# First feed-forward block of an S5 layer kernel: w1 loaded by rows, 14 sums open at once, a norm's scales on GpSimd

## The chip, the cores and the metric

One core of one Trainium2 chip runs the whole program. The metric is the device time of one execution in microseconds (us): the median of three runs of the kernel before is 155.63 us (155.48 to 155.71). TensorE (PE) multiplies matrices and adds into eight PSUM banks, VectorE (DVE), ScalarE (ACT) and GpSimd (POOL) do the elementwise work, and SyncE (SP) issues nearly all DMAs. Each engine takes its own instructions in order; between engines an instruction waits on semaphores.

## The reference

The input x is 2048 tokens of 448 values, in bf16. Everything starts from one layer norm without weights and runs in two branches:

```python
xn  = layernorm(x)                                  # eps 1e-5
# branch A: a diagonal complex state space model
dt  = exp(log_dt);  Lam_bar = exp(dt * Lam)         # Lam = Lambda_re + 1j Lambda_im, 448 states
Bu  = xn @ ((Lam_bar - 1) / Lam * B).T              # complex, 448 x 448
h_t = Lam_bar * h_(t-1) + Bu_t                      # over the 2048 tokens
s   = 2 * Re(h @ C.T) + xn * Dskip
# branch B: a second layernorm on xn and a feed-forward block
g   = silu(gelu(layernorm(xn) @ w1 + b1) @ w2 + b2) # w1: 448 x 1792, w2: 1792 x 448
out = x + s * g
```

## The kernel before

The tokens are cut into four groups `g` of 512. A group has two blocks `b` of 256 tokens, and a block two parities `par`: row pairs 2p and 2p+1 lie on partition p, so that a tile is 128 partitions by 448. All of x, w1, w2, B and C stay in SBUF.

Work is recorded as tasks in a class `Plan`: a task is a list of instructions of one engine with the names of what it reads and writes. `link` turns the names into dependencies, and `emit` issues the tasks in a list written out by hand, `ORDER` (numbers stand for tasks without a tag, names for tagged ones); `SECOND` lists the tasks that go to the second of their two possible engines. Before a task's first instruction `emit` puts the semaphore waits of all its dependencies. DMAs are tasks too, nearly all on SP's queue (a few on ACT's); copies are issued on line 90, transposing DMAs on line 89.

The head, up to 19.6 us, is what the change is about:

- `ldw1` (L333) loads w1 in four column chunks, `CH = ((0, 4), (4, 4), (8, 4), (12, 2))` in units of 128 columns. Rows 0 to 383 go as 3 x 128 partitions, the last 64 rows as a second DMA. w2 comes in four chunks of rows, the bias b1 in four small loads (`b1b`), w1's last partition 64 of row chunk 3 holds b1 for the first group.
- 28 matmuls of the identity on itself (L828) keep TensorE busy until there is data. They wait for GpSimd's memsets.
- `first_norm` (L386 to L405) does block 0: statistics on VectorE (L393, L394), the scale by Ln and Exp on ScalarE (L396), the normalised block (L398), TensorE transposes (L401) with five dummy matmuls behind them (L403), and copies out of PSUM into `xn2T` (L405). The nine small matmuls of `parameters` (L480 to L484), which turn the state parameters to columns, come ahead of these.
- For block 1 of group 0, `ln_stats` (L379, L383) and `ln_scale` (L412) run on VectorE: ten small operations (L422 to L432) take an inverse square root by two Newton steps. `ln_apply` (L448) normalises, TensorE transposes (L464), VectorE copies (L470).
- `mm1_half` (L742) multiplies one block by w1, two column tiles f at a time: for each f the four row chunks d one after another, 8 matmuls of 128x128 by 256 tokens, into a pair of banks (0/1, 2/3, 4/5 in turn), followed by one gelu on ScalarE (L754). Seven pairs for block 0, then seven for block 1.
- `mm2` (L757) follows: 14 matmuls for each (block, parity), which wait for all four w2 chunks before the first; then b2 (L765) and silu (L766).

From group 1 on, `mm1` (L724) does the w1 product for both blocks at once, 512 tokens wide, with row tiling: two products of 64 rows each stand side by side in the array (L728), and the 64 rows left over are copied to both halves. Its gelu is L738. `bu` (L651) multiplies by the transposed B (`BT`, product L654), the scan follows on VectorE (L679), and `ym` (L783) multiplies the states by C (products L792, L795 and L798), then the product with g (L801), the skip and the residual (L804), and the store. `xn2T` and `xnT` of the later groups, `BT` and `Cr` (C transposed) are made by transposing DMAs on SP's queue.

GpSimd and ScalarE work out the angles and powers of the scan (L500 to L519 on GpSimd) between 6 and 16 us. For groups after the first, `ln_scale` runs on GpSimd as two add-multiplies (L422, L423), a power of -0.5 (L424), a multiply and a change of sign (L425, L426), all with one instruction for 4 or 8 columns.

Of the kernel before, what the change touches and what calls it, by code (L numbers as in the profile page):

```python
# [9 lines left out]
BF = dt.bfloat16  # L10
# [7 lines left out]
class Task:  # L18
# [3 lines left out]
    __slots__ = ("eng", "ins", "reads", "writes", "sem", "idx", "deps", "chain", "alts", "tag")  # L22

    def __init__(self, eng, ins, reads, writes, sem):
        self.eng, self.ins, self.reads, self.writes, self.sem = eng, ins, tuple(reads), tuple(writes), sem
        self.deps = set()
        self.chain = False
        self.tag = None
        self.alts = [(eng, ins)]
# [7 lines left out]
class Plan:  # L37
# [55 lines left out]
    def link(self):  # L93
        last, readers = {}, {}
        for t in self.tasks:
            for k in t.reads:
                if k in last:
                    t.deps.add(last[k])
            for k in t.writes:
# [12 lines left out]
    def emit(self):  # L112
# [8 lines left out]
        for t in order:  # L121
# [3 lines left out]
            need = {}  # L125
            for d in t.deps:
                sem, val = done[d]
                if need.get(sem, 0) < val:
                    need[sem] = val
            for sem, val in need.items():  # L130
                if seen.get(sem, 0) < val:
                    eng.wait_ge(self.sems[sem], val)
                    seen[sem] = val
            for k, fn in enumerate(t.ins):
                last = fn(eng)
# [26 lines left out]
10 0 18 22 1 19 23 20 16 15 88 2 21 11 3 9 27 26 12 8 17 14 13 89 24 5 7 90 25 6 4 91 28 96 29 45 97 30 92 98 93 46 31 99 94 47 48 63 103 95  # L162
53 100 32 49 101 54 50 102 33 51 52 106 114 64 44 65 55 108 105 B0 56 116 115 B1 107 109 B2 57 117 58 B3 42 118 38 110 120 39 119 40 144 122
111 121 104 41 60 112 DH 36 123 69 126 59 113 34 67 37 124 305 127 35 154 304 43 128 125 148 132 152 129 66 306 134 307 149 133 310 308 309
311 155 130 193 153 135 312 156 138 131 195 146 140 157 159 139 158 136 147 160 161 275 137 68 316 BF 61 317 62 72 70 167 313 318 73 141 272
314 74 71 169 75 76 287 W0 168 276 W1 170 82 281 171 83 77 273 162 78 410 84 173 86 163 413 W2 284 278 183 315 196 150 184 164 282 417 174
283 412 W3 288 80 79 411 277 185 414 165 H10 279 166 143 415 H12 416 274 177 285 418 364 151 518 517 H11 519 365 187 368 172 366 145 369 175
H13 191 516 81 319 367 H15 419 186 521 176 370 422 320 374 523 178 390 188 371 522 233 85 87 179 289 189 375 H16 520 286 322 420 192 180 423
H14 323 234 524 393 376 424 235 377 190 372 236 421 237 373 321 199 378 200 238 241 528 324 242 203 182 197 239 181 204 H21 198 243 201 H20
240 202 472 425 470 529 325 471 207 247 525 194 473 250 381 251 326 530 244 526 249 245 205 527 252 H23 206 261 H24 142 209 248 476 246 379  # L170
478 253 255 262 208 256 327 210 257 266 258 259 211 328 221 263 267 219 264 260 265 329 212 268 477 220 213 382 254 222 223 384 225 269 226
224 214 229 227 280 215 230 330 270 228 H26 216 231 383 428 217 232 331 218 334 290 333 479 335 387 291 385 386 332 293 388 426 389 H22 427
294 295 297 391 336 292 339 482 298 474 299 483 338 300 337 344 475 429 H30 342 430 353 341 H25 301 296 564 340 496 343 480 565 H31 392 347
345 302 H33 354 355 531 348 394 566 349 481 499 350 358 271 570 359 431 360 346 567 484 351 352 356 361 362 432 380 396 571 433 534 397 395
399 532 434 435 533 400 401 403 303 436 439 440 487 398 441 402 404 485 406 535 448 488 437 536 489 490 438 497 357 449 442 446 498 445 493
447 444 443 451 453 454 363 537 494 491 495 450 492 H32 538 407 459 H34 464 486 460 568 408 461 465 H36 462 569 539 466 452 405 455 500 463
409 576 540 467 H35 593 468 572 501 456 574 469 573 457 458 541 575 502 542 577 545 546 543 503 581 544 547 553 552 554 550 505 582 578 506
583 555 504 507 590 508 548 509 551 549 557 591 579 556 587 510 558 559 580 560 512 561 584 592 562 513 563 511 514 599 588 515 589 596 600
585 594 586 595 603 597 598 601 602 611 604 607 612 605 613 606 608 614 609 610
""".split()]  # L180
SECOND = [int(k) if k.isdigit() else k for k in """
142 143 144 145 146 147 149 161 167 169 197 199 205 207 221 223 227 229 231 284 285 286 391 392 394 395 419 423 428 496 501 524 525 529 590 591 592 594 595 613 W0
# [12 lines left out]
def bass_recurrent_scan__ssm_conv_s5__mixer_channel_mlp__prompt_kernel(  # L195
# [18 lines left out]
    with ExitStack() as es:  # L214
# [3 lines left out]
        ident = SB("ident", [128, 128])  # L218
        mhalf = SB("mhalf", [128, 1, 1], F32)
# [70 lines left out]
        with nc.Block():  # L290

            S0 = -100
            pool(lambda e: e.memset(ident[:], 1.0), [], ["ident"], 0.2, 3 * PINNED)
# [39 lines left out]
            def ldw1(c, prio):  # L333
                a, w = CH[c][0] * 128, CH[c][1] * 128
# [9 lines left out]
            for c in (1, 2, 3):  # L344
                ldw1(c, S1 + 3)
# [487 lines left out]
            for par in range(2):  # L833
                ln_apply(0, 1, par, 1, "only dve", 2 * PINNED + 4)
# [86 lines left out]
```

## Time and profile before

| what | value |
|---|---|
| median of three runs | 155.63 us (155.48 to 155.71) |
| profiled execution | 155.18 us, span 153.1 us, 2.1 us outside the span |
| granted TensorE clock, mean | 1.00 |
| PE busy | 148.4 us of the span, 97% |
| DVE, ACT, POOL busy | 86%, 67%, 31% |
| first matmul, first w1 product, first w2 product | 1.42, 6.50, 19.60 us |
| w1 chunks landed | 6.24, 7.97, 9.49, 10.20 us |
| w2 chunks landed | 16.42, 17.58, 18.77, 19.55 us |
| one transposing DMA on SP's queue | 1.2 to 1.3 us of issue, landing about 3 us after its start |

A row of the timeline gives the start and length in us, the engine, the line, the operation, what is written and read, the tile, the number of instructions, and, in square brackets, the idle time before it with what ended it. The chain of waits goes back from the last instruction to what released each step. The waits list says for each engine and line how long it stood idle and for whom. The profiled execution lies 0.45 us under the median, so a time worked out from its rows is taken against 155.18 and then set to the median.

### The profile page before, as it was taken

Reading aid. Unit: us, or ns where it says so; the run is one execution under the profiler, and the core shown is the slowest. Engines: PE = TensorE matmul, PEld = TensorE weight load, DVE = VectorE, ACT = ScalarE, POOL = GpSimd, SP = SyncE. Lnnn points to the kernel's source line nnn. Section 1 sums busy time; section 2 is a strip of 40 time slices with the busy share of each in tenths; the row PEclk is TensorE's granted clock in tenths of the full one; section 3 lists DMA queues with packets and bytes.
Section 4 is the critical chain, followed back from the end, with each engine's and each line's share of the span. In section 5 each row is a group of like instructions: output and inputs, shape, how many; then the busy total and the mean of one; then the engine's idle time right before and its main releaser. Section 6 shows DMA issues by size and latency. Waiting matters only on the chain.

```text
span 153.1 us, 3017 instructions
## 1 busy us (share of the span) xinstructions
PE 148.4 (97%) x1079; PEld 89.9 (59%) x1079; DVE 131.3 (86%) x275; ACT 102.5 (67%) x175; POOL 47.3 (31%) x122
## 2 busy tenths in 40 slices
PE   6999999999999999999999999999999999999992
PEld 6899945454575555755544556665555665555551
DVE  5879999999988999999859998349699539999784
ACT  3876959999885688798993599841419987244110
POOL 6465896374520004700000079000512920000001
PEclk9999999999999999999999999999999999999999
DMA  4998999996859553000003310042300100010103
GB/s 115 311 259 268 349 175 238 211 187 130 160 88 175 88 103 69 0 2 0 4 1 59 84 40 0 0 96 84 62 2 0 62 0 4 0 62 0 60 0 120
DMA packets 31512, 14.04 MB, mean 92 GB/s; under 512 B 25733, under 2 KB 31113, under 8 KB 31498
## 3 DMA queue, kind: packets, MB, share of 16 engines
q1 hardware_dynamic: 31344, 13.80, 39.5%
q8 instruction: 8, 0.13, 0.4%
q10 hardware_dynamic: 154, 0.06, 0.1%
q14 instruction: 6, 0.05, 0.1%
HBM read 6.20 MB, written 1.84 MB: 53 GB/s over the span
## 4 chain that ended last, share of the span: by engine, by line
PE 85%; SPq 6%; DMA 5%; issue 1%; DVE 1%
PE psum L762 28%; PE psum L728 22%; PE psum L654 15%; PE psum L792 13%; SPq L90 6%; DMA w_sb<-in_B_w_dram 5%; PE psum L795 4%; PE psum L636 3%; PE psum L798 1%; PE psum L642 1%; DVE t L801 0%; DVE tmp L804 0%; PE psum L638 0%; PE psum L644 0%
## 5 line engine op out<-in xcount | busy, mean ns | idle before, releaser
L762 PE MATMUL psum<-w_sb,gT 128*128 128x448 bf16 x224 | 44.3, 353 | 0.1
L728 PE MATMUL psum<-xn2T,w_sb 64*128 64x512 bf16 x294 | 33.9, 378 | 0.0
L762 PEld LDWEIGHTS psum<-w_sb,gT 128*128 128x128 bf16 x224 | 21.8, 98 | 19.8 <-DMA w_sb<-in_B_w_dram 0.4
L738 ACT ACTIVATE gT<-psum,b1f 128x512 bf16<-128x512 f32 x42 | 26.0, 687 | 6.9 <-PE psum L728 6.7
L728 PEld LDWEIGHTS psum<-xn2T,w_sb 64*128 64x128 bf16 x294 | 15.6, 109 | 16.1 <-issue 3.0
L654 PE MATMUL psum<-xnT,BT 128*128 128x256 bf16 x196 | 24.1, 273 | 0.0
L654 PEld LDWEIGHTS psum<-xnT,BT 128*128 128x128 bf16 x196 | 18.4, 98 | 6.5 <-issue 3.3
L766 ACT ACTIVATE g_sb<-o 128x448 bf16<-128x448 f32 x16 | 9.1, 572 | 12.2 <-DVE o L765 12.1
L801 DVE TENSOR_TENSOR t<-psum,g_sb 128x448 bf16<-128x448 f32 (+2 forms) x17 | 10.0, 591 | 5.9 <-PE psum L795 2.8
L679 DVE TENSOR_TENSOR_SCAN s_f<-cw,cur,v_sb 128x256 f32<-128x256 f32 x21 | 14.9, 737 | 0.1
L693 POOL TENSOR_TENSOR cwk<-s_f,ang 128x3 f32<-128x3 f32 x3 | 1.4, 470 | 43.3 <-DVE s_f L679 43.3
L748 PE MATMUL psum<-xn2T,w_sb 128*128 128x256 bf16 x112 | 12.6, 273 | 0.3 <-DVE xn2T L405 0.3
L748 PEld LDWEIGHTS psum<-xn2T,w_sb 128*128 128x128 bf16 x112 | 11.9, 111 | 0.7 <-issue 0.4
L792 PE MATMUL psum<-CZ,h_sb 128*128 128x448 bf16 x56 | 11.9, 353 | 0.0
L765 DVE TENSOR_TENSOR o<-psum,b2bc 128x448 f32<-128x448 f32 x16 | 9.7, 614 | 1.7 <-PE psum L762 1.7
L792 PE MATMUL psum<-CQ,h_sb 128*128 128x448 bf16 (+2 forms) x54 | 10.5, 332 | 0.0
L683 ACT ACTIVATE s_b<-s_f 128x1536 bf16<-128x1536 f32 x4 | 5.9, 1485 | 6.7 <-DVE s_f L679 6.7
L658 ACT ACTIVATE u_sb<-psum 128x512 bf16<-128x512 f32 x12 | 7.2, 598 | 4.6 <-PE psum L654 4.6
L448 DVE TENSOR_SCALAR xn_sb<-x_all,lnw 128x448 bf16<-128x448 bf16 (+1 forms) x30 | 9.9, 364 | 0.3
L754 ACT ACTIVATE gT<-psum 128x512 bf16<-128x512 f32 x14 | 8.2, 592 | 2.7 <-PE psum L748 2.7
L804 POOL TENSOR_TENSOR tmp<-t,xr 128x192 bf16<-128x192 bf16 x1 | 0.5, 548 | 26.3 <-DVE t L801 26.3
L792 PEld LDWEIGHTS psum<-CZ,h_sb 128*128 128x128 bf16 x56 | 5.3, 98 | 5.1 <-issue 0.5
(160 smaller groups left out, 236.9 us busy)
## 6 DMA issues: line engine op xcount, KB each, us to landing
out_dram<-tmp SPq DMA_DIRECT2D x7, 224.0 KB, 1.9
x_all<-in_A_x_dram SPq DMA_DIRECT2D x3, 448.0 KB, 4.7
w_sb<-in_B_w_dram SPq DMA_DIRECT2D x3, 448.0 KB, 7.3
w_sb<-in_B_w_dram SPq DMA_DIRECT2D x3, 384.0 KB, 4.4
Bn<-in_A_B_im_dram SPq DMA_DIRECT2D x1, 336.0 KB, 8.5
Bn<-in_A_B_re_dram SPq DMA_DIRECT2D x1, 336.0 KB, 8.7
x_all<-in_A_x_dram SPq DMA_DIRECT2D x2, 112.0 KB, 2.1
x_all<-in_A_x_dram SPq DMA_DIRECT2D x1, 224.0 KB, 2.7
```

The source lines that it names most:

```text
L90: return e.dma_start(out_ap, in_ap)
L448: on = [("dve", [lambda e, o=o, i=i: e.tensor_scalar(o, i, rs, nb, op0=ALU.mult, op1=ALU.add) for o, i in pairs], 0.4, 0.12), ("act", [lam ...
L654: fns = [lambda e, r=r, m=m, d=d: e.matmul(psum[:, 4, r * NK:(r + 1) * NK], BT[:, m, d, :], xnT[:, gx, d, :], start=(d == 0), stop=(d == 6 ...
L679: dve(lambda e, i=i, ri=ri, init=init: e.tensor_tensor_scan(s_f[:, i, ri, :], col(R2, i).to_broadcast([128, NK]), v_sb[:, i, ri, :], init, ...
L728: return lambda e: e.matmul(psum[:, b0 + k, :], w1_sb[halves[h], d, fcol(2 * j + k)], rhs[halves[h], d, :, :], start=first and d == 0, sto ...
L738: act([lambda e, k=k: e.activation(gT[:, gb, 2 * j + k, :], psum[:, b0 + k, :], ACT.Gelu_apprx_tanh, bias=b1f[:, 2 * j + k:2 * j + k + 1]) ...
L748: fns = [lambda e, k=k, d=d: e.matmul(psum[:, banks[k], :].rearrange("p (r c) -> p r c", r=2)[:, :, cs], w1_sb[:, d, fcol(2 * j + k)], rhs ...
L762: fns = [lambda e, fi=fi: e.matmul(psum[:, bk, 0:D], gT[:, gb, fi, q * 128:(q + 1) * 128], w2_sb[:, fi, :], start=(fi == 0), stop=(fi == N ...
L765: dve(lambda e: e.tensor_tensor(o2[:, ob, :], psum[:, bk, 0:D], b2bc[:], ALU.add), [f"ps{bk}", "b2bc"], [f"oo{ob}"], 0.62, prio - 76)
L766: act(lambda e: e.activation(g_sb[:, gs, :], o2[:, ob, :], ACT.Silu), [f"oo{ob}"] + (["silu"] if g == 0 else []), [f"g{gs}"], 0.58, prio - ...
L792: fns = [lambda e, k=k: e.matmul(psum[:, bk, c0:c1], h_sb[:, hb, k, k0:k0 + 128], cm[:, k, c0:c1], start=(k == 0), stop=False) for k in ra ...
L801: dve(lambda e: e.tensor_tensor(t3[:, fb, c0:c1], psum[:, bk, c0:c1], g_sb[:, gs, c0:c1], ALU.mult), [f"ps{bk}", f"g{gs}"], [f"t3{fb}_{c0} ...
```

## The change

- A task can have waits at a later instruction than its first (`late`), and dependencies that need no wait since they lie ahead on the same in-order engine (`behind`).
- w1 is loaded by row chunks d of 128, 128, 128 and 64 rows, each in two column halves of 8 and 6 tiles, so that one row on a partition is 2 KB or 1.5 KB in place of 1 KB. b1's columns come in two loads instead of four.
- The dummies are 9 matmuls of 512 columns on a zeroed tile `still`, which VectorE sets first. Parity 0's transposes go ahead of the parameter matmuls, parity 1's behind them.
- Block 0's product runs row chunk by row chunk: first d=0 for parity 0 and parity 1 apart (8 column tiles), then whole, then d=1, d=2 and d=3. 14 sums of 256 columns stand open in banks 0 to 6, two in each bank, and the seven gelus come only behind d=3. Block 1's transposes use bank 7, its products take banks (j + 7) mod 8.
- `second_norm` takes block 1's scales of group 0 from VectorE to GpSimd: an add-multiply and a power for what the apply needs, then a second pair for the other norm. VectorE applies as (x - mean) * r.
- The first group's `mm2` waits for w2's first chunk only, and for the others before its instructions 4, 8 and 12.
- The last store of 256 columns goes by ACT's queue, that of 192 columns by SP's; before it was the other way about.
- `ORDER` and `SECOND` are new as a whole. In SP's queue the x copy, two 64-row copies of B (`Bn`) and a copy of C (`Cs`) stand among the transposes; before, the `Bn` copies went ahead of all of them. TensorE runs the row-tiled products (L728) in 10 stretches between other products, where there were 11.

```diff
+            for i, keys in t.late.items():
+                t.ldeps[i] = {last[k] for k in keys}
...
             for k, fn in enumerate(t.ins):
+                for d in t.ldeps.get(k, ()) if k else t.deps - t.behind:
...
-            def ldw1(c, prio):
-                a, w = CH[c][0] * 128, CH[c][1] * 128
-                ld("sp", w1_sb[:, 0:3, a:a + w], dram_ap(B_w1, a, [[F, 128], [128 * F, 3], [1, w]]), [f"w1_{c}"], 384 * w * 2, prio, dur=0.55)
-                ld("sp", w1_sb[0:64, 3, a:a + w], dram_ap(B_w1, 384 * F + a, [[F, 64], [1, w]]), [f"w1r_{c}"], 64 * w * 2, prio)
+            HC = ((0, 8), (8, 14))
+            def ldw1(d, h):
+                n, (a, z) = (128, 128, 128, 64)[d], HC[h]
+                ld("sp", w1_sb[0:n, d, a * 128:z * 128], dram_ap(B_w1, d * 128 * F + a * 128, [[F, n], [1, (z - a) * 128]]), [f"w1_{d}{h}"], n * 256 * (z - a), 0, dur=0.55)
...
+            def second_norm():
+                q = slice(1, 4, 2)
+                kb.add("pool", [lambda e: e.tensor_scalar(w1, var, 1.0 + LN_EPS, LN_EPS * LN_EPS, op0=ALU.mult, op1=ALU.add),
+                                lambda e: e.tensor_tensor(r1, w1, half(2), ALU.pow)], ["mv0_1", "mv0_3", "mhalf"], ["r1b"], dur=0.7, lat=0.15, chain=True)
+                kb.add("pool", [lambda e: e.tensor_scalar(w0, var, 1.0, LN_EPS, op0=ALU.mult, op1=ALU.add),
+                                lambda e: e.tensor_tensor(r0, w0, half(2), ALU.pow),
+                                lambda e: e.tensor_tensor(n0, mean, r0, ALU.mult),
+                                lambda e: e.tensor_scalar(n0, n0, -1.0, None, op0=ALU.mult)],
+                       ["mv0_1", "mv0_3", "mhalf"], ["lnw0_1"], dur=1.4, lat=0.15, chain=True)
...
+            def mm1_first():
+                def part(d, f, r):
+                    return lambda e: e.matmul(bank_of(f, f // 2)[:, r, :], w1_sb[:, d, fcol(f)], rhs[:, d, r, :], start=(d == 0 and f % 2 == 0 and r.start == 0), stop=(d == 3 and f % 2 == 1))
...
+                run(0, 0, 8, slice(0, 1), "Q0")
+                run(0, 0, 8, slice(1, 2), "Q1")
+                run(0, 8, 14, slice(0, 2), "Q2")
+                for d in (1, 2):
+                    for h in range(2):
+                        run(d, *HC[h], slice(0, 2), f"Q{2 * d + 1 + h}")
+                for j in range(7):
+                    run(3, 2 * j, 2 * j + 2, slice(0, 2))
+                    mm1_gelu(j, 0, j)
...
-                pe(fns, [f"gT{gb}_{fi}_{b}" for fi in range(NF)] + [f"w2_{c}" for c in range(4)], [f"ps{bk}"], 2.66, prio)
+                pe(fns, [f"gT{gb}_{fi}_{b}" for fi in range(NF)] + [f"w2_{c}" for c in range(1 if g == 0 else 4)], [f"ps{bk}"], 2.66, prio)
+                if g == 0:
+                    kb.tasks[-1].late = {w: [f"w2_{c}"] for c, w in LATE}
...
-            pe([lambda e: e.matmul(psum[:, 3, 0:128], ident[:, :], ident[:, :], start=True, stop=True) for _ in range(28)],
-               ["ident"], ["ps3"], 2.8, 3 * PINNED)
+            pe([lambda e: e.matmul(psum[:, 3, :], still[:, :], still[:, None, :].to_broadcast([128, 4, 128]), start=True, stop=True) for _ in range(9)],
+               ["still"], ["ps3"], 2.8, 3 * PINNED)
```

In the kernel after, lines have moved: the dummies are L881, transposes L416 (dummies L418), parameter matmuls L506 to L510, block 0's product L777, block 1's transposes L490 and product L805, mm2 L813, `mm1` from group 1 on L754, `bu` L680.

167 lines of the change are left out of this document (91 added, 76 removed).

## The prediction

> **What bounds the kernel now.** I read the page first, then the chain of waits with its last pieces in order of time, then the waits by engine, then TensorE's, GpSimd's and SyncE's rows in time.
>
> ```profile
> PE 148.4 (97%) x1079; PEld 89.9 (59%) x1079; DVE 131.3 (86%) x275; ACT 102.5 (67%) x175; POOL 47.3 (31%) x122
> PE   6999999999999999999999999999999999999992
> PE 85%; SPq 6%; DMA 5%; issue 1%; DVE 1%
> ```
>
> PE is busy in every slice but the first and last. Nothing else sets the end: only PE work taken out, a PE wait removed, or a PE wait created moves the time. The chain's first 19.6 us are queue and DMA, up to one landing:
>
> ```profile
> 11.23 8.32 DMA w_sb<-in_B_w_dram
> 19.55 0.05 issue
> 19.60 10.77 PE psum L762 x56
> ```
>
> Yet TensorE's rows in time show that it was working until then:
>
> ```profile
> 1.42 3.17 PE L828 MATMUL psum<-ident 128*128 128x128 bf16 x28 [1.42 <-POOL mhalf L314]
> ...
> 6.50 4.53 PE L748 MATMUL psum<-xn2T,w_sb 128*128 128x256 bf16 x40 [0.28 <-DVE xn2T L405]
> 10.99 0.62 PE L464 MATMUL psum<-ident,xn_sb 128*128 128x128 bf16 x8
> 11.45 8.03 PE L748 MATMUL psum<-xn2T,w_sb 128*128 128x256 bf16 x72
> 19.60 1.12 PE L762 MATMUL psum<-w_sb,gT 128*128 128x448 bf16 x5
> ```
>
> So the last w2 chunk (19.55) delays the second product (L762) by hardly 0.25 us (the page gives "DMA w_sb<-in_B_w_dram 0.4" for its weight load). The earlier w1 landings (7.97, 9.49, 10.20 for chunks 1 to 3) are just ahead of use. The stage up to 19.60 holds little slack to win.
>
> **The change, part by part.** Times are of the profiled execution: 155.18 = span 153.1 + 2.1 outside. It lies 0.45 below the median, 155.63.
>
> *Warm-up.* 28 matmuls of 128 columns become 9 of 512 (107 ns per 128 columns, so 0.43 each, 3.85 in all). They wait for VectorE's memset, not GpSimd's L314 at 1.42; start 1.2 (bounds: 0.9, just after the program's start, and 1.42). They end near 5.06, as before (4.5 plus 0.5 of parameter matmuls).
>
> *Order of transposes.* Parity 0: 5.06 to 5.29, its 5 dummies to 5.57, the nine parameter matmuls (4.52 to 5.01 before, 0.5) to 6.07, parity 1 from 6.07. The first product starts after the dummies, 6.58 (6.50 before); parity 1 is copied by 6.9 (row L405, 0.42 to 0.47), for its half at 7.04. Parameters come 1.1 later (5.57 against 4.52); behind them is GpSimd's angle chain, costed below.
>
> *First block, d by d.* The same columns: 16 half-width products at 0.058 (128 columns in rows L401 and L464 take 0.057) are 0.93, to 7.51; 36 of 256 columns at 0.1093 (4.53 less the last drain, over 40) are 3.93, to 11.44; eight transposes 0.46, to 11.90; the 68 left 7.43, to 19.33. That is 0.27 before 19.60. Row chunks must come in order. At the rate of before's 1-KB rows (chunk 0 landed at 6.24, chunk 1, 458 KB, at 7.97: 265 KB/us) after the first x (3.33): d0 at 4.3 and 5.0, block 1's x 5.9, d1 at 6.8 and 7.5, d2 at 8.5 and 9.2, d3 at 9.7 and 10.1. They are needed at 6.58, 7.51, 8.17, 9.04, 9.70, 10.79, 10.57 and, for the second half of d3, about 12: never under 0.9 spare, and I expect longer rows to be faster.
>
> *Clock.* L828 runs 128 columns in 107 ns, L401 at 5.01 in 57. The fast rate came after some 3.5 us of unbroken PE work. The new start is as unbroken and as early, so the first block runs at the fast rate; if it came 0.5 later, that would cost 0.25 at most.
>
> *Gelus.* All of block 0's now wait for d=3, so seven (0.60 each) start from 12.1 in place of 7.3. ScalarE ends them near 16.5 to 18 and the second product needs them at 19.3; bank releases have 0.2 to 0.7 us to spare.
>
> *Scales of block 1.* Ten VectorE rows (8.03 to 10.02, 2.0 us) go. GpSimd does add-multiply, power, then two applies on VectorE (0.40 each); behind them stand a second power and two small rows. No row shows a power of 128x2. Nearest:
>
> ```profile
> 16.29 2.10 POOL L424 TENSOR_TENSOR lnw<-lnw,mhalf 128x8 f32<-128x8 f32 x1
> 18.46 0.20 POOL L425 TENSOR_TENSOR lnw<-lnmv,lnw 128x8 f32<-128x8 f32 x1
> 18.75 1.18 POOL L426 TENSOR_SCALAR lnw<-lnw 128x8 f32<-128x8 f32 x1
> ```
>
> Ends: 0.20 (a plain small op) and 2.10 (no shrinking with columns; a second row took 1.67). I take 0.65: a fixed 0.2 and the rest by columns. Statistics end at 8.6, so applies end near 10.8, transposes are due at 11.44: 0.6 spare. GpSimd's angle chain, behind both powers, feeds ScalarE's sines, which stand before the gelus; there hardly anything is spare. So each 0.1 us on a power costs about 0.2 at PE; at 0.65, nothing. Below nothing it cannot go: PE is continuous there.
>
> The L426 row speaks against the move: 1.18 us beside VectorE's L571 (18.59 to 19.82), 0.31 for the same form at 34.71. One such block would hold the scales by about 0.9 (1.18 less 0.31): a rival below. Around 8.6 to 10.8 VectorE's rows are short (0.2 to 0.6), and GpSimd's rows there took 0.37 and 0.35 instead of 0.25, so I take no block. [...] The 2.0 us that VectorE saves lie beside PE and buy nothing alone: its last needed work of the head, the copy of the eight transposes (0.69), only follows PE.
>
> *w2.* The queue issues the chunks earlier, b1 in two loads instead of four; they land by about 17.5 and the waits (before instructions 0, 4, 8 and 12 of each product) find them there: the 0.25 is in the 0.27. Were the last chunk as late as 19.55 again, the first that needs it comes at 21.6 (19.33 and twelve at 0.191): still nothing.
>
> *New order.* The row-tiled products (L728) run in 10 stretches, not 11. A stretch costs about 0.2 in joins: chain rows give L654 x14 1.53 apart from L728 and 1.63 to 1.65 beside it, and L728 0.1 fixed. So -0.2. Small PE waits (about 0.2 in all after 19.6) may go or come: zero.
>
> *SyncE's queue.* Before, both 64-row Bn loads went ahead of all transposes. Now three copies (x, Bn, Bn) and one Cs copy lie among them. SyncE before:
>
> ```profile
> 23.90 1.31 SPq L89 DMA_TRANSPOSE xn2T<-xn_sb  x1
> 25.25 0.58 SPq L90 DMA_DIRECT2D x_all<-in_A_x_dram  x1
> 25.88 2.43 SPq L89 DMA_TRANSPOSE xnT<-xn_sb  x1
> ```
>
> A transpose holds the queue 1.31 us, lands 3 later, and took 2.43 behind a copy: 1.16 extra (bounds 0, as after the x copy at 18.39, and 1.16). From the first xn2T (21.24 before; two xnT now ahead of it, so near 22.5), ten transposes (13.1) and four copies (2.4) go before the BT that the third Bu product (L654 before) waits for: issued 38.0, landed near 41.2. PE wants it at 43.7 (30.1 + the same stretches). Spare: 2.0 to 2.5. With 1.16 at three places, 3.5, PE waits 1.0 to 1.5. I take none or one: the x copy alone also had it before, and the kernel lost nothing. [...]
>
> *Tail.* The last 256-column store goes by ScalarE's queue, the 192-column one by SyncE's; rows of both show 1.56 from issue to landing. Zero.
>
> Sum: -0.27 - 0.2 = -0.47, so 154.7 profiled, 155.15 at the median; I write **155.1**.
>
> **The rivals.**
> *SyncE's alternation (slower).* Each of the two Bn copies and the Cs copy delays the transpose behind it by 1.16; the third Bu product and the next xn2T wait. For it: the 2.43 row, and another of 2.48 at 15.85 behind copies. Against: the Cs copies at 49.77 followed transposes with no gap. It decides when the extras pass about 2.2 us. At three: +1.2 to +1.6 on -0.47, so 156.3 to 156.8.
>
> *The power does not shrink, or GpSimd is blocked (slower).* The head waits for xn2T or for the gelus' banks. Break-even with -0.47 is a power of 0.9. One block of 0.9 gives 156.0; 2.10 gives 19.33 + 2.8, so 157.9.
>
> *The 0.47 comes back.* The gelus, bunched, release banks late, or PE starts 0.3 later at the head: 155.5 to 155.7.
>
> **How the numbers follow.** A measurement of this kernel can tell about 0.2% (0.31 us) from no change. Forecast (155.1, its own range 154.4 to 155.5): 0.50. Alternation: 0.25. GpSimd: 0.12. Returned: 0.13. Faster by over 0.2% (below 155.32): the forecast's 0.50 less 0.05 at its edge, plus 0.03 of the others, 0.48. Within: 0.17, that edge and most of the returned. Slower: 0.35, the two slower rivals less a little. The range goes down to 154.4 (small waits of 0.2 gone, joins cheaper still) and up to 156.9, past the alternation; it leaves out the powers of over 1.4.
>
> **What the profile after would show.** Right: L777 starts near 6.6, L813 near 19.3 with no releaser; powers of 128x2 near 0.65; weight waits at L813 gone; the third L680 stretch with no idle. Wrong: a row "PE psum L777/L805 <- ..." of over 0.3, powers over 0.9, SyncE transposes of 2.4 at the Bn copies, with "PE L680 <- DMA BT" behind them, or gelus (ScalarE) still running at 19 us.

## The result and the profile after

The kernel after takes 157.69 us (157.44 to 157.80, four runs) against 155.67 for the kernel before in the same runs: a ratio of 1.0118 [1.0083, 1.0154]. It is slower by 1.2%, outside the predicted range. Its profiled execution is 157.80 us, span 156.1, 1.7 outside; before it was 155.18, span 153.1. Single executions at a lower granted clock, or more than 1.5% above the fastest of their kernel, are left out of all medians and ratios below.

The page after, first busy times, then TensorE by slices, then the shares of the chain that ended last:

```profile
PE 149.6 (96%) x1068; PEld 88.5 (57%) x1068; DVE 124.4 (80%) x249; ACT 104.5 (67%) x179; POOL 57.3 (37%) x136
PE   7989999999998979999999999999999999999992
PE 48%; DVE 17%; ACT 12%; POOL 8%; DMA 6%; issue 3%; SPq 3%; POOLq 0%; DVEq 0%; ACTq 0%
```

TensorE is no longer busy in every slice: dips have come (the third, thirteenth and fifteenth slices), and VectorE, ScalarE and GpSimd, which had hardly a part in the chain, now hold 37% of it. The waits of TensorE after (us in total, times, longest) name the new gaps:

```profile
PE psum L680 <- ACT u_sb L688: 1.0, 1, 1.0
PE psum L777 <- DMA w_sb<-in_B_w_dram: 0.7, 1, 0.7
PE psum L754 <- DMA xn2T<-xn_sb: 0.6, 1, 0.6
```

They stand in TensorE's rows in time after. The head:

```profile
6.78 4.41 PE L777 MATMUL psum<-xn2T,w_sb 128*128 128x128 bf16 x44
11.92 1.04 PE L777 MATMUL psum<-xn2T,w_sb 128*128 128x256 bf16 x8 [0.74 <-DMA w_sb<-in_B_w_dram]
12.80 0.61 PE L490 MATMUL psum<-ident,xn_sb 128*128 128x128 bf16 x8
...
20.72 0.54 PE L813 MATMUL psum<-w_sb,gT 128*128 128x448 bf16 x2
```

and 27 to 35 us further on, in a stretch where TensorE never stood before:

```profile
48.07 3.21 PE L754 MATMUL psum<-xn2T,w_sb 64*128 64x512 bf16 x28 [0.60 <-DMA xn2T<-xn_sb]
...
55.78 1.69 PE L680 MATMUL psum<-xnT,BT 128*128 128x256 bf16 x14 [0.98 <-ACT u_sb L688]
```

The second product (L813) starts at 20.72, before at 19.60: +1.12. Then come the waits of 0.60 and 0.98. The last product ends at 153.13 against 150.22, +2.91, so these three are 2.70 of it. The time outside the span is 0.4 less.

Why the two later waits? VectorE's and GpSimd's rows after, at the end of the head:

```profile
22.85 1.26 DVE L477 TENSOR_SCALAR xn_sb<-x_all,lnw 128x448 bf16<-128x448 bf16 x4 [1.39 <-POOL lnw L458]
```
```profile
19.68 0.20 POOL L454 TENSOR_SCALAR lnw<-lnmv 128x4 f32<-128x4 f32 x1
...
20.24 1.95 POOL L456 TENSOR_TENSOR lnw<-lnw,mhalf 128x8 f32<-128x8 f32 x1
```

The scales of group 1, which began at 15.71 before, begin at 19.68, and VectorE's applies of group 1 at 22.85 instead of 19.96. Busy time by window (the window and its length; then PE, PEld, DVE, ACT and POOL busy, clock, DMA share, GB/s), of before and then of after:

```profile
2.50:23.00 20.50, 20.09 (x185) 17.32 (x184) 18.07 (x56) 15.35 (x32) 13.95 (x49) 1.00 1.04 270
23.00:47.00 24.00, 24.00 (x184) 13.40 (x183) 22.92 (x59) 22.05 (x36) 11.50 (x21) 1.00 0.89 168
```
```profile
2.50:23.00 20.50, 19.66 (x175) 15.73 (x173) 13.65 (x39) 13.00 (x30) 13.49 (x46) 1.00 1.07 274
23.00:47.00 24.00, 24.00 (x183) 13.13 (x183) 23.62 (x59) 21.97 (x35) 12.41 (x29) 1.00 1.09 167
```

From 2.5 to 23 us VectorE has done 4.4 us less. Only 2.0 of that was taken off it; the rest comes later. From 23 to 47 it is busy for 95% before and 98% after, so it has little room to catch up.

### The profile page after: what moved, and what is told of

It is laid out like the page before. It is cut to its first block, busy times and chain, and to the rows that moved or that the text cites. A ratio compares the mean times of both kernels' runs of the same rounds, so it can differ in the third digit from the quotient of the medians.

```text
span 156.1 us, 2980 instructions
## 1 busy us (share of the span) xinstructions
PE 149.6 (96%) x1068; PEld 88.5 (57%) x1068; DVE 124.4 (80%) x249; ACT 104.5 (67%) x179; POOL 57.3 (37%) x136
## 3 DMA queue, kind: packets, MB, share of 16 engines
HBM read 6.20 MB, written 1.84 MB: 52 GB/s over the span
## 4 chain that ended last, share of the span: by engine, by line
PE 48%; DVE 17%; ACT 12%; POOL 8%; DMA 6%; issue 3%; SPq 3%; POOLq 0%; DVEq 0%; ACTq 0%
PE psum L813 12%; PE psum L754 11%; PE psum L845 10%; PE psum L680 7%; DMA w_sb<-in_B_w_dram 4%; PE psum L848 3%; PE psum L662 3%; DVE Bn L624 3%; DVE s_f L705 3%; SPq L92 2%; DVE tmp L622 2%; DVE lnst L394 2%; POOL lnw L456 2%; ACT gT L764 2%; DMA Bn<-in_A_B_im_dram 2%
## 5 line engine op out<-in xcount | busy, mean ns | idle before, releaser
L813 PE MATMUL psum<-w_sb,gT 128*128 128x448 bf16 x224 | 44.2, 352 | 0.0
L754 PE MATMUL psum<-xn2T,w_sb 64*128 64x512 bf16 x294 | 33.8, 378 | 0.7 <-DMA xn2T<-xn_sb 0.6
L813 PEld LDWEIGHTS psum<-w_sb,gT 128*128 128x128 bf16 x224 | 21.8, 98 | 19.8 <-issue 0.3
L754 PEld LDWEIGHTS psum<-xn2T,w_sb 64*128 64x128 bf16 x294 | 15.9, 109 | 16.5 <-issue 2.0
L680 PE MATMUL psum<-xnT,BT 128*128 128x256 bf16 x196 | 24.1, 273 | 1.0 <-ACT u_sb L688 1.0
L680 PEld LDWEIGHTS psum<-xnT,BT 128*128 128x128 bf16 x196 | 18.3, 98 | 7.7 <-issue 2.0
L829 POOL TENSOR_TENSOR xr<-xd,g_sb 128x448 f32<-128x448 bf16 x4 | 4.5, 1118 | 43.3 <-DVE tmp L857 19.9
L705 DVE TENSOR_TENSOR_SCAN s_f<-cw,cur,v_sb 128x256 f32<-128x256 f32 x21 | 15.6, 770 | 0.1
L478 ACT ACTIVATE xn_sb<-x_all,lnw 128x448 bf16<-128x448 bf16 (+1 forms) x16 | 10.4, 679 | 1.7 <-POOL lnw L458 1.6
L845 PE MATMUL psum<-CQ,h_sb 128*128 128x448 bf16 (+2 forms) x54 | 10.5, 332 | 0.0
L797 ACT ACTIVATE gT<-psum 128x512 bf16<-128x512 f32 x14 | 7.6, 606 | 4.1 <-PE psum L777 3.5
L477 DVE TENSOR_SCALAR xn_sb<-x_all,lnw 128x448 bf16<-128x448 bf16 (+1 forms) x24 | 8.6, 391 | 1.6 <-POOL lnw L458 1.4
L394 DVE BATCH_NORM_STATS2 lnst<-x_all 128x6 f32<-128x448 bf16 x14 | 8.2, 613 | 0.1
## 6 DMA issues: line engine op xcount, KB each, us to landing
Bn<-in_A_B_im_dram SPq DMA_DIRECT2D x1, 336.0 KB, 10.1
```

Source lines behind the costliest of these rows:

```text
L394: dve([lambda e, b=b, par=par, q=q: e.bn_stats(lnst[:, q, :], x_all[:, 2 * g + b, par, :])], [f"x{2 * g + b}"] + (["xmT0p1"] if (g, b) == ...
L477: on = [("dve", [lambda e, o=o, i=i: e.tensor_scalar(o, i, rs, nb, op0=ALU.mult, op1=ALU.add) for o, i in pairs], 0.4, 0.12), ("act", [lam ...
L478: ("act", [lambda e, o=o, i=i: e.activation(o, i, ACT.Identity, bias=nb, scale=rs) for o, i in pairs], 0.75, 0.2)]
L680: fns = [lambda e, r=r, m=m, d=d: e.matmul(psum[:, 4, r * NK:(r + 1) * NK], BT[:, m, d, :], xnT[:, gx, d, :], start=(d == 0), stop=(d == 6 ...
L705: dve(lambda e, i=i, ri=ri, init=init: e.tensor_tensor_scan(s_f[:, i, ri, :], col(R2, i).to_broadcast([128, NK]), v_sb[:, i, ri, :], init, ...
L754: return lambda e: e.matmul(psum[:, b0 + k, :], w1_sb[halves[h], d, fcol(2 * j + k)], rhs[halves[h], d, :, :], start=first and d == 0, sto ...
```

## The experiments

All ratios are to the kernel before, run beside each kernel on the same chip (155.69 to 155.84 at the median). The theories, by the letters that the expectations use: *W*, the w1 rows land late and delay the head; *G*, block 1's scales on GpSimd hold its angle chain, and with it group 1's scales; *A*, one small angle activation on ScalarE, now behind the first gelu, does; *D*, VectorE starts late after the head (by G, A or W) and has no slack later; *O*, the new order behind the head makes waits whatever the head does; *F*, a fetch of TensorE's program holds a transposing DMA; *Q*, ScalarE's order around 52 us. Two more have no letter: SyncE's alternation of copies and transposes (the prediction's rival), and the scales of group 3, which the new `SECOND` put on GpSimd (in before they ran on VectorE, to 45.4).

**The kernel after again**, unchanged.

> The changed kernel once more, for a second trace. If w1's late row chunks are a property of these loads, the last one lands at 12.0 to 12.4 us again and TensorE waits 0.5 to 0.9 us for it; if it was an accident of one execution, it lands near 10 and the second product starts near 19.6. Time 157.4 to 157.8 in the first case, about 1 us less in the second.

157.96, ratio 1.0136 [1.01, 1.0173]. The head waits for w1 twice (0.67 and 0.48), xn2T 1.20, u_sb 0.40. The waits are the same, their sizes change by up to 0.6 us from one execution to the next, and single gaps are to be read so.

**Block 1's scales back on VectorE**, and the same with the angle activation ahead of the first gelu.

```diff
-                kb.add("pool", [lambda e: e.tensor_scalar(w1, var, 1.0 + LN_EPS, LN_EPS * LN_EPS, op0=ALU.mult, op1=ALU.add),
...
+                kb.add("dve", fns, ["mv0_1", "mv0_3"], ["r1b", "lnw0_1"], dur=2.05, lat=0.12, chain=True)
```

> Block 1's scales of group 0 go back to VectorE as ten small operations. Theory G (GpSimd, 3.4 us of norm rows ahead of its angle chain, makes group 1's scales late, 19.68 against 15.71, and with them VectorE and SyncE): the scales start near 17.6, the waits of 0.6 and 0.98 at 48 and 56 us shrink, 156.0 to 156.8. Theory A (ScalarE: the angle activation L538 stands behind a gelu that needs d=3 and starts at 14.2, so GpSimd would only wait for it): GpSimd idles until 14.4 and the time stays at 157.3 to 157.8. Theory W (the supply of w1 alone): no change either, 157.3 to 157.8.

157.74, 1.012 [1.0089, 1.0151]. mm2 starts at 19.82, but GpSimd, freed of its eight rows, only stands waiting, as its timeline shows:

```profile
13.54 0.33 POOL L538 TENSOR_SCALAR ang<-ang 128x16 f32<-128x16 f32 x1 [2.84 <-ACT ang L547]
...
18.77 0.20 POOL L463 TENSOR_SCALAR lnw<-lnmv 128x4 f32<-128x4 f32 x1
```

It waits for one small activation that stands behind the first gelu, and the gelus now all come late: of the two, A holds. So:

```diff
-112 41 124 65 113 126 125 122 36 120 147 114 57 34
+112 41 124 65 113 126 57 125 122 36 120 147 114 34
```

> As the run before, and ScalarE's angle activation L538 goes ahead of the first gelu. Theories G and A together: GpSimd's chain runs from about 10.5, group 1's scales start when their statistics are there, near 17.6, 2 us earlier; waits at 48 and 56 us go or halve: 155.8 to 156.6. Theory G alone: the same as the run before. Theory W: no change, 157.3 to 157.8.

157.46, 1.0131 [1.0081, 1.0181]. The scales of group 1 start at 17.28 and now wait for VectorE's statistics, no longer for GpSimd's queue; but w1 costs 0.81 in this execution and the later waits stay (0.45 and 1.00). The 155.8 to 156.6 that G and A together had forecast did not come: 2.4 us on group 1's scales alone gain nothing that can be measured.

**Group 3's scales to VectorE.**

```diff
-SECOND = ... 500 525 532 ...
+SECOND = ... 500 525 532 ... 524
```

> The scales of group 3 go back to VectorE, as they were; nothing else. If the wait of 0.98 us at 55.8 comes from these five GpSimd rows (46.7 to 52.3, two of them 1.2 and 1.4 us long beside VectorE), it goes: 156.5 to 157.0. If ScalarE is only late with all its work, the wait stays and the time too, 157.3 to 157.8; if VectorE's ten rows push the scan, it gets slower by up to 1.

158.14, 1.0147 [1.0126, 1.0168]. The xn2T wait is gone, yet VectorE's longer work comes back as 1.31 at the second product (through ScalarE's gT) and 0.37. So the place of these scales alone is not the cause: wherever they go, something waits.

**The last w1 rows over 128 partitions**: the same bytes in the same two DMAs.

```diff
+                if d == 3:
+                    m = (z - a) * 64
+                    ld("sp", w1_sb[:, 3, a * 128:a * 128 + m], dram_ap(B_w1, 320 * F + a * 128, [[F, 128], [1, m]]), [f"w1_{d}{h}"], n * 256 * (z - a), 0, reads=["w1b"], dur=0.55)
+                    return
```

> Changed kernel; the last row chunk of w1 is written to 128 partitions with half the bytes on each, in place of 64 (w1's last 64 rows are then wrong in the products). If the packets between 9 and 11.5 us take twice their time because these two loads reach only half of the partitions, the last chunk lands 0.6 to 1.0 us earlier, near 11, and packets of 9 to 11 us are back to 84 and 65 ns at the median. If the engines are slowed by something else, it lands at 11.3 to 12.5 as before. Time about the same, 157.2 to 157.8, since the stages behind have waits of their own.

157.54, 1.0112 [1.0074, 1.015]. The two halves land at 9.49 and 10.24 (11.79 and 12.22 after), and packets at 9 to 11 us take the usual time, where they took 1.8 to 2.6 times as long after. The head of this kernel, TensorE's rows in time:

```profile
6.85 4.99 PE L781 MATMUL psum<-xn2T,w_sb 128*128 128x128 bf16 x52
11.68 0.61 PE L494 MATMUL psum<-ident,xn_sb 128*128 128x128 bf16 x8
...
15.04 5.40 PE L809 MATMUL psum<-xn2T,w_sb 128*128 128x256 bf16 x48 [0.57 <-ACT gT L801]
20.28 0.92 PE L817 MATMUL psum<-w_sb,gT 128*128 128x448 bf16 x4
```

All 52 products run without a break, so W is settled for its place. Behind it stands the next lateness: a bank that its gelu releases 0.57 late, and the transposes at 49.00, which are 1.45 late in this execution. So the time stays where it was.

**w1 by whole rows**, one DMA for each row chunk instead of two halves.

```diff
-                n, (a, z) = (128, 128, 128, 64)[d], HC[h]
+                n, (a, z) = (128, 128, 128, 64)[d], (0, 14)
```

> Changed kernel; each row chunk of w1 comes as one load of whole rows (3584 bytes) in place of two halves. If half rows are what slows the engines, the last chunk lands near 10 to 10.5 and TensorE does not wait for it; if it is the number of engines out of step or the last 64 rows, it lands at 11.3 to 12.5 again. Time 157.0 to 157.8.

157.24, 1.0113 [1.0077, 1.0149]. The 64 rows still land at 12.13, and packets are still about twice as long (3584 bytes: 271 ns at the median from 9 to 10 us, 140 otherwise): the partitions matter, not the length of a row.

**Old order behind the new head, and new order behind the old head.** The lists are joined at one task.

```diff
-# ORDER from task 272 on: this kernel's own list
+# ORDER from task 272 on: the other kernel's list
```

> The changed kernel up to its first w2 product (all tasks ahead of it in the new order, on their new engines); every task behind that in the order, and on the engines, of the kernel before. If the head makes the loss (w1 late by 1.1 us, GpSimd's angle chain late), the loss stays: 157.0 to 157.8. If the new order behind it makes it (waits of 0.6 and 1.0 us at 48 and 56 us), those waits are gone: 156.2 to 156.8, before plus the head's 1.1. If both are only spare used up twice, about 156.8.

> The counterpart: the kernel before up to its first w2 product, every task behind it in the new order and on the new engines. If the new order alone makes waits of 1.6 us: 156.9 to 157.4. If it needs the late head (VectorE and GpSimd 3 to 4 us behind) to make them, it gives what its one stretch of row-tiled products fewer promised: 155.3 to 155.8.

> The new head with the old order behind it, for an undisturbed trace. Its time was 156.4 to 157.7. Theory D: VectorE starts group 1's norms 2 to 3 us late here too, and TensorE waits for VectorE or ScalarE somewhere between 23 and 60 us, 0.5 to 1 us in all, on top of the head's 1.1; if nothing but the head is late, the first w2 product starts near 20.7 and no wait of over 0.3 follows.

New head, old order: 157.35, 1.0088 [1.0051, 1.0125], and again 157.72, 1.0108 [1.002, 1.0197]. In the repeat the second product starts at 20.71, and waits of 0.75 (VectorE, at 26.93) and 0.66 (xn2T, at 33.04) follow; those at 48 and 56 us are gone. Old head, new order: 160.09, 1.0307 [1.0236, 1.0378], with waits of 0.85, 2.20 (VectorE, at 27.68) and 1.40 (u_sb, at 57.06). The first wait behind the seam may be the seam's own, so the shares of head and order can't be split this way. What holds is that the new head costs even under the old order.

**More instructions ahead of the same work**: 36 dummies of 128 columns for 9 of 512.

```diff
-            pe([lambda e: e.matmul(psum[:, 3, :], still[:, :], still[:, None, :].to_broadcast([128, 4, 128]), start=True, stop=True) for _ in range(9)],
+            pe([lambda e: e.matmul(psum[:, 3, 0:128], still[:, :], still[:, :], start=True, stop=True) for _ in range(36)],
```

> Changed kernel; the warm-up as 36 matmuls of 128 columns in place of 9 of 512: the same columns and time, 27 matmuls (54 instructions) more in TensorE's program. Theory F (a transposing DMA in flight stalls 1.1 to 1.7 us when a 16-KB piece of TensorE's program is fetched, at 45.3 in the changed kernel, on the two transposes that TensorE waits for at 48.07): the fetch moves to about 42.5, hits an earlier transpose, whose delay the queue passes on, or one that has time to spare: the wait at 48 goes or halves, and the one at 55.8 grows by as much, 157.0 to 157.7. If the fetch has nothing to do with it, the stall stays at 45 to 47 us. No theory expects over 0.6 of gain.

158.57, 1.0187 [1.0148, 1.0225]. Queue 8 of the page, "instruction", moves eight packets of 16 KB. In after one comes for every 204 to 272 of TensorE's instructions in the trace, and so they are read here as pieces of TensorE's program. One is under way for 1.15 us from 45.28 on, while SyncE's xn2T transposes are being written; the DMA view of 45 to 46.6 us has it as

```profile
q8 instruction: 1, 0.02, 4.5%
```

With 27 more matmuls ahead it came at 42.82, and the xn2T wait was gone. (The other wait grew to 1.61, and 0.8 us more lay outside the span. A ninth fetch, at 157.67 and so behind the span's end, stands in this trace alone; whether it makes the 0.8 was not tried.) The same holds over the executions with the new order:

```
fetch begins  45.28 46.00 44.92 44.82 46.28 44.24 46.90 44.53 46.66 | 42.82 47.35 47.45 48.72 49.09
xn2T wait      0.60  1.20  0.54  0.45  1.45  0.52  1.32  0.47  0.59 |   none in any of these
```

**The mended head, new order**: w1 over 128 partitions, scales on VectorE, angle activation first (the three edits above together).

> Changed kernel in its new order, with three faults of the head out at once: w1's last row chunk over 128 partitions (its last 64 rows are then wrong in the products), block 1's scales on VectorE, ScalarE's angle activation ahead of the first gelu. Theory D (VectorE, full from 23 to 49 us in both kernels, starts that stretch 2 to 3 us late because the head leaves it idle, and transposes, scales of group 3 and TensorE follow): group 1's norms start near 20 in place of 22.85, VectorE reaches the scan's first product 2 us earlier (47 against 48.95), the wait at 55.8 falls under 0.4, time 155.6 to 156.5. Theory O (the new order is bad behind the head whatever the head does): waits of 1.0 to 1.6 us stay, 156.9 to 157.5.

156.68 (156.51 to 156.90, nine runs), 1.0054 [1.0032, 1.0075]: half of the loss is back. mm2 starts at 19.24, and only one wait of over 0.3 is left behind it; TensorE, then GpSimd, then ScalarE in time:

```profile
54.66 1.69 PE L693 MATMUL psum<-xnT,BT 128*128 128x256 bf16 x14 [1.84 <-issue]
```
```profile
45.55 0.46 POOL L467 TENSOR_SCALAR lnw<-lnmv 128x4 f32<-128x4 f32 x1 [1.23 <-DVE lnmv L406]
...
46.69 1.75 POOL L469 TENSOR_TENSOR lnw<-lnw,mhalf 128x8 f32<-128x8 f32 x1
48.52 1.16 POOL L470 TENSOR_TENSOR lnw<-lnmv,lnw 128x8 f32<-128x8 f32 x1
49.76 1.42 POOL L471 TENSOR_SCALAR lnw<-lnw 128x8 f32<-128x8 f32 x1
```
```profile
51.30 2.22 ACT L491 ACTIVATE xn_sb<-x_all,lnw 128x448 bf16<-128x448 bf16 x4 [1.35 <-POOL lnw L471]
...
54.19 0.38 ACT L701 ACTIVATE u_sb<-psum 64x256 bf16<-64x256 f32 x1
```

Statistics (VectorE) at 45.5, scales (GpSimd) to 51.2, applies (ScalarE) to 53.5, then the copies of Bu's sums that free TensorE's banks, to 54.57: four engines in a row. In the kernel before, these copies ran at 50.93, with no scales of group 3 ahead of them, and its statistics of group 3 were done 5.7 us earlier:

```profile
39.55 0.18 DVE L383 BATCH_NORM_AGGREGATE lnmv<-lnst 128x2 f32<-128x6 f32 x1
```

VectorE's own lateness is small here: its applies of group 1 start at 20.29 (before 19.96), the scan's first product at 47.80 (before 46.94). So most of the 5.7 us is the place of these rows in the new list. D had said that this wait would fall under 0.4, O that waits of 1.0 to 1.6 would stay; the wait stayed, as by O, and the time lies between the two forecasts. The new order has a share in the late waits, beside the head.

**The same head edits by other means.** The 64 rows on ScalarE's queue under the old order (scales and angle activation as in the run before, not shown again):

```diff
-                ld("sp", w1_sb[0:n, d, a * 128:z * 128], dram_ap(B_w1, d * 128 * F + a * 128, [[F, n], [1, (z - a) * 128]]), [f"w1_{d}{h}"], n * 256 * (z - a), 0, dur=0.55)
+                ld("act" if d == 3 else "sp", w1_sb[0:n, d, a * 128:z * 128], dram_ap(B_w1, d * 128 * F + a * 128, [[F, n], [1, (z - a) * 128]]), [f"w1_{d}{h}"], n * 256 * (z - a), 0, dur=0.55)
```

> A candidate that computes all of the reference: the new head up to the first w2 product, w1's last 64 rows issued early on ScalarE's queue, scales on VectorE, the angle activation ahead of the first gelu, and the old order from the first w2 product on. Theory D: no waits over 0.3 behind 20 us, and the first w2 product near 19.6: 155.3 to 156.2, about the kernel before. Theory O: the same, since the order is the old one. If it is over 156.6, something else in the head costs VectorE its time.

158.96, 1.0191 [1.0128, 1.0253]: the 64 rows landed at 7.14 and 8.22, in time. But issuing them holds ScalarE for 1.17 us from 2.52 on, ahead of its first norm's scale: TensorE waits 1.08 for block 0's first transposes, and its first 16 products, from 8.65 on (6.78 after), take 0.107 each in place of 0.056. So mm2 starts at 22.18, and the run tells nothing of D or O.

**The kernel before with the scales of block 1 on GpSimd**, nothing else.

```diff
-            ln_scale(0, 2 * PINNED + 3, (1,))
-            for par in range(2):
-                ln_apply(0, 1, par, 1, "only dve", 2 * PINNED + 4)
+            second_norm()
```

> The kernel before with one part of the change alone: block 1's scales of group 0 by GpSimd's powers. Theory D and G: powers of 0.73 us, GpSimd's angle chain 3.4 us later, group 1's scales start near 19 in place of 15.71, VectorE idles 1 to 2 us more before 23 us, and TensorE gets waits of 0.3 to 1.5 us behind: 156.0 to 157.2. If the move alone is harmless: 155.5 to 155.9.

156.67 (156.56 to 156.82, seven runs), 1.0042 [1.0011, 1.0072]. Slower by itself: VectorE's busy time from 2.5 to 23 us falls from 18.07 to 15.30, more than the 2.0 taken, its applies of group 1 start at 21.50 (19.96 before), and TensorE stands for 0.54 in the second product:

```profile
26.30 5.46 PE L784 MATMUL psum<-w_sb,gT 128*128 128x448 bf16 x28 [0.54 <-PE psum L784]
```

The row names TensorE itself, which had been done by then; that it waits for a bank that VectorE empties late is the author's reading. Not all of the difference between the two traces is VectorE's. The first product starts at 7.00 and the second at 20.30 (6.50 and 19.60 before), since w1 and w2, whose loads were not touched, landed 0.6 to 0.7 later in this execution. So of 1.5 us between the traces, 0.54 is put on VectorE.

**Group 3's applies behind the copies of Bu** (two applies and a transpose moved in the list), on the mended head and on the kernel after; and a version that computes all of the reference, with the 64 rows sent between the others.

```diff
-242 472 528 206 470 194 243 239 529 204 378 240 530 207 250 473 248 251 325 471 244
+242 472 206 470 194 243 239 204 378 240 207 250 473 248 251 325 471 528 529 530 244
```

> The kernel with the mended head (w1's last row chunk over 128 partitions, so its last 64 rows are wrong in the products), and group 3's two norm applies on ScalarE, with the transpose behind them, after the copies of the fourth state product and two pairs of gelus. Theory Q (ScalarE's order: the applies wait for GpSimd's scales and hold the copies that free the bank): the wait of 1.84 us at 54.7 goes, 154.7 to 155.3, under the kernel before, which is what was forecast for the change. Theory D alone (VectorE late): the wait comes back at the next product that needs VectorE's results, 156.2 to 156.8.

> The changed kernel with this one move and nothing else. Theory Q: the wait of 0.98 us at 55.8 goes, the 0.6 for the transposes at 48 and the 1.1 of the head stay: 156.5 to 157.0. Theory D: no change, 157.3 to 157.9.

> A candidate that computes all of the reference: the changed kernel with scales on VectorE, the angle activation ahead of the first gelu, the applies of group 3 later, and w1's last 64 rows loaded in between the other row chunks, so that fewer engines write to the same 64 partitions at once. If the parts add up and w1 is 0.3 to 0.8 late still: 155.1 to 156.0. If the loads of 64 partitions cost the same wherever they stand: 155.6 to 156.4.

156.48 (155.52 to 157.85), 1.0037 [0.9997, 1.0078]; 158.01, 1.0116 [1.0044, 1.0189]; 156.77, 1.0041 [1.0004, 1.0078], over both of its forecasts. The wait at 54.66 (55.78 in the kernel after) is gone in all three, and yet the first two take, within their wide spread, the time of the kernels that they were made from, 156.68 and 157.69. TensorE's rows of the first show why:

```profile
46.78 3.22 PE L767 MATMUL psum<-xn2T,w_sb 64*128 64x512 bf16 x28 [0.52 <-DMA xn2T<-xn_sb]
...
58.76 1.50 PE L675 MATMUL psum<-CQ,Bn 128*128 128x448 bf16 x7 [0.56 <-DVE CQ L637]
```

VectorE's `CQ` is late next, and a fetch at 44.24 lies on the xn2T transposes. Q alone falls: it had forecast 154.7 to 155.3. That ScalarE's order only chose where VectorE's lateness is paid is a reading of these rows.

**Less for VectorE**: statistics of groups 2 and 3 over 64 columns, on the kernel after and on the mended head.

```diff
-x_all[:, 2 * g + b, par, :])], [f"x{2 * g + b}"]
+x_all[:, 2 * g + b, par, 0:D if g < 2 else 64])], [f"x{2 * g + b}"]
```

> The changed kernel; the statistics of groups 2 and 3 are taken over 64 columns in place of 448 (so their norms are wrong): eight VectorE rows of 0.61 us shrink to about 0.15, some 3.6 us less work between 23 and 47 us. Theory D (VectorE's lateness makes the waits): the wait of 0.98 at 55.8 goes and the one at 48 goes or stays within 0.5; the head's 1.1 stays: 156.1 to 156.8. If ScalarE, GpSimd or the transposes alone make them: 157.2 to 157.8.

> The same with the mended head (w1's last row chunk over 128 partitions, scales on VectorE, angle activation first; w1's last 64 rows and the norms of groups 2 and 3 are wrong). Theory D: no wait over 0.5 behind 20 us: 154.8 to 155.4, what was forecast for the change. If not: 156.3 to 156.8, as with the mended head alone.

156.79, 1.0082 [1.0048, 1.0117], and 155.96 (155.71 to 156.33, ten runs), 1.0009 [0.9982, 1.0035]. VectorE's 23 to 47 us fall from 23.62 to 20.37 and from 23.33 to 20.69, and the ratios by 0.0036 (intervals that still overlap) and 0.0045 (intervals that barely touch), some 0.6 and 0.7 us. In the first the u_sb wait of 0.98 is gone and an xn2T wait of 0.59 stays, nearly as D had said (it had allowed 0.5). So VectorE's load has a share in the late waits. The second did not reach the 154.8 to 155.4 expected of it: one wait of 1.01 stays at 54.20, with the same chain over GpSimd (the rows of 1.16 and 1.42 again) and ScalarE ahead of it. How that would divide between GpSimd's rows, ScalarE's order and the place of group 3's statistics in the list was not tried.

No version that computes the reference beat the kernel before.

## Why the prediction was wrong, by its steps

The forecast was -0.47 on the profiled execution, the result +2.62. Two steps failed: the landing of w1's row chunks, and the waits behind 19.6 us, which the text took as zero.

- **The w1 row chunks ("never under 0.9 spare"): the step that failed first.** The landings were summed at the 265 KB/us of a load over 128 partitions. (Worked out again at that rate, d3 lands at 9.88 and 10.26, and the least spare is 0.7.) After, d1 landed at 8.23 and 8.75 (6.8 and 7.5 summed), just in time, d2 at 10.07 and 11.13 (8.5 and 9.2 summed), d3 at 11.79 and 12.22 (9.7 and 10.1). The sum needed d3's first half at 10.57, so TensorE waited 0.74; its 44 products up to there took 4.41 instead of 3.99, d2's first half being late as well. With 0.20 for the later start (6.78, not 6.58) that makes the head's 20.72 instead of 19.33. The row order made the whole head depend on the 64-row chunk, in two DMAs on 64 partitions each; over 128 partitions they landed at 9.49 and 10.24, as summed, and d1 and d2 were earlier too (7.21 to 9.12). In before the 64-row loads were there too, but each was a seventh of its chunk, behind the other rows.
- **Waits behind 19.6 us ("may go or come: zero"): the step that failed second.** They are 0.60 and 0.98, more than the head's loss. The runs show three shares and don't divide them: a fetch of TensorE's program that lies on the xn2T transposes (the wait goes when the fetch moves), VectorE's load (less of it takes 0.6 to 0.7 us off), and the new order (1.84 stays with the head mended). How much is whose stays open.
- **The head's sum over columns: right; the clock: right in this execution.** With w1 on time, the angle activation first and the scales back on VectorE, mm2 starts at 19.24, 19.33 in the sum; the granted clock is 1.00. TensorE's fast rate (0.056 us for 128 columns, 0.107 ahead of it) began at 5.6 us after. In the profiled executions of two later kernels (group 3's applies later, and less for VectorE, both on the kernel after) it began only at 10.5, and they took 1.3 to 1.4 us more than their kernel's median; what delays it was not tried.
- **The gelus ("0.2 to 0.7 to spare"): too small a margin.** Hidden after by w1; with w1 on time a bank came 0.57 late, and no longer once the scales and the angle activation were put back.
- **The scales on GpSimd: size right, cover wrong.** The powers took 0.73 and 0.75 (0.65 taken), below the 0.9 at which the rival decides, and nothing at block 1 waited. But the text costed the move at nothing because VectorE's 2.0 us "lie beside PE and buy nothing". It saw the angle chain behind the powers ("hardly anything is spare") and followed it to the gelus, but not to group 1's scales, which stand behind it: eight rows of 3.4 us ahead of the chain, and the angle activation behind the first gelu. Of the 4 us by which group 1's scales are late, the two edits give back 0.9 and 1.5; the rest is that VectorE's statistics come later. VectorE then had idle time in the head and little to make it up later (95 to 98% busy from 23 to 47 us, where the text went by its 86% over the span). On the kernel before, the part alone costs 0.42%, of which 0.54 us are put on VectorE by the author's reading of its trace.
- **SyncE's alternation (the rival): wrong mechanism, near the right place.** Copies ahead of transposes cost nothing that the rows show. SyncE's rows after:

```profile
38.81 1.30 SPq L91 DMA_TRANSPOSE BT<-Bn  x1
40.15 0.60 SPq L92 DMA_DIRECT2D h_sb<-in_A_C_im_dram  x1
40.80 1.23 SPq L91 DMA_TRANSPOSE BT<-Bn  x1
42.07 2.69 SPq L91 DMA_TRANSPOSE xn2T<-xn_sb  x2
44.87 2.01 SPq L91 DMA_TRANSPOSE BT<-Bn  x1
```

  The 1.23 follows a copy; the 2.01 follows none, and lies on the fetch at 45.28. The 2.43 at 25.88 and the 2.48 at 15.85 before, from which the 1.16 was taken (2.43 less 1.31 is 1.12), lie beside fetches too (26.62 and 15.73). The xn2T wait of 0.60 goes with that fetch: with more dummies VectorE is nearly as late (22.49 at group 1's applies, 22.85 after) and the wait is gone.
- **GpSimd blocked (the rival): rows of such a length came, elsewhere.** Not in the small rows at 9 us, but in group 3's scales, which the new order put on GpSimd: 1.16 and 1.42 where the same rows took 0.21 and 0.25 in other groups (L457 and L458, their shortest). They end at 50.83 and 52.34, 0.06 and 0.10 behind VectorE's rows of 128x1536 (to 50.77 and 52.24); that these block them was read from the rows, not tested. The text priced the new order by TensorE's stretches and SyncE's queue and passed over the line of `SECOND` that moved these scales. Putting them back alone gains nothing (158.14).
- **The new order's one stretch fewer (-0.2): not seen.** From mm2's start to the last product, less the named waits, before took 130.62 and after 130.83.
- **w2 and the tail at nothing: right.** TensorE does not wait at L813 for w2, and the span ends 2.9 us behind the last product in both.

## What to carry to other kernels

When work is taken off an engine that isn't the bound, look at how busy that engine is stage by stage and at everything queued behind the work on the engine that gets it; an engine at 95% has little room to make up a late start, and the price can appear far behind (here at 26 us for a head that ends at 20). When a load is cut anew, time its landing from a load of the same number of partitions (here the last piece landed at 12.22 over 64 partitions and at 10.24 over 128), above all where an accumulation makes all the work wait for the last piece. When a wait moves from engine to engine as one reorders, look both at the engine that feeds them all and at where its rows stand in the list: here less work on VectorE helped, and group 3's statistics stood 5.7 us later with VectorE hardly late. And a new order is a risk to be priced by its waits, not only by its joins.

## What was not expected of the hardware

- While w1's last 64 rows are loaded into partitions 0 to 63, packets take about twice as long: 84 ns for 2048 bytes and 65 ns for 1536 become 161 to 216 and 119 to 155 (medians of half microseconds, 9 to 11 us), and the 3584-byte packets of the loads behind 257 to 332 in place of 140. With the same bytes over 128 partitions packets take the usual time, and from 9 to 12 us 377 GB/s are moved in place of 215. The 16 DMA engines also finished one load of w1 up to 2.5 us apart (3.6 in the second execution, 0.7 before), d1's loads over 128 partitions (2.0 and 1.6) among them, for which no run shows the reason.
- Beside a 16-KB fetch of TensorE's program some packets of a DMA transpose that is under way take long: at the fetch of 45.28 in the kernel after, 22 of them take 1.12 to 1.59 us, where the median is 0.018 and from 41 to 49.3 us no other takes over 0.10. At the fetch of 30.60 it is 22 packets of 0.93 to 1.27 us, while TensorE itself has no idle there. A fetch is not all that goes with such packets: in the same kernel some of 0.5 to 1.1 us stand at 24 to 27 and near 37 us too, with no 16-KB fetch beside them. In the run with 27 matmuls more ahead of the transposes, the fetch came at 42.82 in place of 45.28 and the xn2T wait of 0.60 was gone; so here the number of matmuls went with whether a transpose was late.
